# An earlier in-place sum, other banks for the queries, and half of an older head's PV between a query group and its scores

## The chip, the cores and the metric

The kernel runs on one core of a Trainium2 chip. The metric is device time in microseconds (us) of one execution, lower is better. Where I speak of "the trace", it is the hardware profiler's record of one execution.

How to read a line of a timeline: start (us from the beginning of the span), length in us, engine, line of the kernel, operation, what it writes <- what it reads, shapes, number of instructions merged into the line, and in brackets how long the engine was idle before it and what ended that. PE is TensorE's matmuls, PEld its weight loads, DVE is VectorE, ACT ScalarE, POOL GpSimd; SPq issues DMAs from SyncE's queue. A bank is one of the eight banks of PSUM, into which TensorE writes. PV is the product of the probabilities with V. "Start to start" is the distance between the starts of two neighbouring matmuls.

## The reference, cut to what matters

```python
x = A_x                                   # 1 x 2048 x 448, bf16
xn = layernorm(x)
q = xn @ wq                               # 16 query heads of 256
k, v = last 512 positions of the caches   # 8 key heads, each serves 2 query heads
p = softmax(q @ k.T / 16)
s = (p @ v) @ wo
g = silu((gelu(xn @ w_gate) * (xn @ w_up)) @ w_down)
return x + s * g
```

The 2048 rows are worked in four chunks of 512. For the attention that makes 64 steps: step m is query head m mod 16 of chunk m // 16, with key head (m mod 16) // 2. "Head 12" below is step 12.

## The kernel before: the parts that matter

Every operation is planned with the buffers that it reads and writes, and each engine runs its own operations in the order in which they were planned. So a line that stands earlier in this program stands earlier in its engine's queue, and a wait at the head of a queue holds everything behind it.

The gate/up part runs over 56 column blocks, two in each step `n`. Between its matmuls it plans sums for the down product, which is computed from seven products instead of eight and needs sums and differences of the activations (`sum_act`, on VectorE). The sum with k = 0 writes its result into the activations themselves, so the first product of the down stage has to wait for it.

```python
ACT_SUMS = [(n, (c, k, i)) for c, i, ns in ((0, 0, (10, 11, 19, 21)), (0, 1, (23, 23, 25, 25)),
                                            (1, 0, (30, 32, 34, 34)), (1, 1, (36, 36, 38, 38)))
            for k, n in enumerate(ns)]
DOWN_AT = {27: 0, 39: 1}
```

The attention, with cuts:

```python
def q_group(n, pairs, more_act=False):        # queries of two heads, into two pairs of banks
    ...
    group(units, 0, QC, True, True)           # 64-row matmuls, two of them side by side
    for i, b in enumerate(pairs):
        act(qT[:, s, 0, :], bank[b], ...)     # one half copied by ScalarE (ACT)
        ...                                   # the other by VectorE (DVE), or by ACT if more_act

def s_mm(m):                                  # scores of head m, four blocks of 128 rows
    for t4 in range(4):
        ...                                   # two matmuls into bank AB[t4]; exp on ACT
        if t4 % 2 == 1:
            ...                               # reciprocal and two scalings on DVE
            dma_t(pT[:, x, t4 // 2, ...], pn[:, y, ...])    # DMA transpose, on the SP queue

def pv(m):                                    # probabilities times V: two halves of four matmuls
    for e in range(2):
        b = BB[m % 2 * 2 + e]
        mms(... va[:, g, j, e * P:(e + 1) * P], pT[:, x, ...] ...)
        ...                                   # copy of the half: e = 0 on ACT, e = 1 on DVE

groups = [0, 4, 12, 18, 26, 34, 42, 50, 58, 64]     # a query group in front of each of these heads
for m in range(64):
    if m in groups:
        for i in range(m, hi, 2):
            q_group(i, ((cur, nxt[::-1], (cur[1], nxt[1])) if three else (cur, nxt) * 2)[p], end)
            ...
            if m == 12 and p == 0:
                for g in range(6, 8): load_k(g)
                for g in range(5, 8): load_v(g)     # V of the last three key heads
                ...                                 # and loads of x and of the gates, on another queue
    s_mm(m)
    ...
    if len(late) == LAG:                      # LAG = 2: PV of head m - 2 follows the scores of head m
        pv(late.pop(0))
    late.append(m)
```

`cur` are the four banks AB of the scores, `nxt` the four banks BB of PV; between two query groups no one else uses them.

The softmax here doesn't subtract the row's maximum and nothing guards it: scores larger than these inputs give would overflow.

Of the kernel before, what the change touches and what calls it, by code (L numbers as in the profile page):

```python
# [168 lines left out]
def bass_recurrent_scan__sliding_block_cached__geglu_ffn__prompt_kernel(  # L169
# [41 lines left out]
    es = ExitStack()  # L211
    with es:
# [158 lines left out]
        groups = [0, Q0, Q0 + QS, Hq + 2] + list(range(Hq + 2 + QS, NQC * Hq, QS)) + [NQC * Hq]  # L371

        def qs(n):
            g = max(i for i in groups if i <= n)
            return n - g + (QS - Q0 if g == 0 else 0)
# [355 lines left out]
        def sum_wt(o, x, y, i):  # L731
# [6 lines left out]
            (48, (o, x, y, i)) for i in range(NB) for o, x, y in ((5, 2, 4), (6, 5, 0), (3, 1, 5))]  # L738
        WD_CASTS = [(16, (j, e, n, i)) for j, e, n in ((0, 0, 0), (4, 0, 1), (2, 1, 1), (1, 1, 0)) for i in range(2)]
        WD_SUMS = [(18, (4, 4, 0)), (20, (5, 2, 4)), (22, (6, 5, 0)), (24, (3, 1, 5))]  # L740
        ACT_SUMS = [(n, (c, k, i)) for c, i, ns in ((0, 0, (10, 11, 19, 21)), (0, 1, (23, 23, 25, 25)),
                                                    (1, 0, (30, 32, 34, 34)), (1, 1, (36, 36, 38, 38)))
                    for k, n in enumerate(ns)]
        DOWN_AT = {27: 0, 39: 1}
        gu_evac(0, 0)
        gu_evac(1, 2)
# [3 lines left out]
        cur, nxt = (0, 2), (4, 6)  # L750
        for n in range(4, NU, 2):
# [6 lines left out]
            cur, nxt = nxt, cur  # L758
# [24 lines left out]
            if n + 1 in DOWN_AT:  # L783
                def norms():
                    for f in (ln_a, ln_a, ln_b, ln_b):
                        f()
                end = down7(DOWN_AT[n + 1], (cur[0], cur[0] + 1, cur[1], cur[1] + 1, nxt[0], nxt[0] + 1),
                            (g2x[:, 0:2, :], g2x[:, 2:4, :]), b_g2x, then=norms if n < 28 else None)
                end(0, 1)
                end(2, 3)  # L790
                cur, nxt = (nxt[1], cur[1]), (cur[0], nxt[0])
# [10 lines left out]
        def q_group(n, pairs, more_act=False):  # L802

            c, h = divmod(n, Hq)
            units = [(b, lambda j, k, i=i: wq[:, k, (h + i) * Dh + j * P:(h + i) * Dh + (j + 1) * P],
                      wqr[:, h + i, :], slice(c * QC, (c + 1) * QC), b_wql[h // HG][:1], b_wql[h // HG][1:], b_xnT[c * 4:c * 4 + 4])
                     for i, b in enumerate(pairs)]
            group(units, 0, QC, True, True)
            for i, b in enumerate(pairs):
                s = qs(n + i)  # L810
                act(qT[:, s, 0, :], bank[b], ACT.Copy, (b_ps[b],), (b_qT[s][0],))
                if more_act and i:
                    act(qT[:, s, 1, :], bank[b + 1], ACT.Copy, (b_ps[b + 1],), (b_qT[s][1],))
                    continue
                K.op("dve", lambda v, s=s, b=b: v.tensor_copy(qT[:, s, 1, :], bank[b + 1]),  # L815
                     (b_ps[b + 1],), (b_qT[s][1],))

        AB, BB = [], []
        LAG = 2
# [20 lines left out]
                    dma_t(pT[:, x, t4 // 2, :, :, :].rearrange("p t j q -> p (t j) q"),  # L840
                          pn[:, y, :, :].rearrange("p t k -> p (t k)"), (b_pn[y],), (b_pT[x][t4 // 2],))

        def pv(m):
            h = m % Hq
            g, x = h // 2, m % NPT
            for e in range(2):
                b = BB[m % 2 * 2 + e]
                mms([(bank[b].rearrange("p (t q) -> p t q", q=P), va[:, g, j, e * P:(e + 1) * P],
                      pT[:, x, :, :, j, :].rearrange("p a t q -> p (a t) q"), j == 0, j == NJ - 1)
                     for j in range(NJ)], [b_va[g]] + b_pT[x], (b_ps[b],))  # L850
                i = 2 * h + e
                if e == 0 or m >= NS - LAG:
                    act(oTh[:, i, :], bank[b], ACT.Copy, (b_ps[b],), (b_oT[i],), scale=WS)
                else:
                    K.op("dve", lambda v, i=i, b=b: v.tensor_scalar(  # L855
                        oTh[:, i, :], bank[b], WS, None, op0=ALU.mult), (b_ps[b],), (b_oT[i],))
# [131 lines left out]
        late = []  # L988
# [8 lines left out]
        for m in range(NS):  # L997
            if m in groups:
                hi = groups[groups.index(m) + 1]
                three = hi - m == 6  # L1000
                for i in range(m, hi, 2):
                    end = m > Hq and m % Hq == LAG
                    p = (i - m) // 2
                    q_group(i, ((cur, nxt[::-1], (cur[1], nxt[1])) if three else (cur, nxt) * 2)[p], end)
                    if m == 0:
                        sum_act(2, 2 + p)
                    if m == Q0 and p == 0:
                        K.reuse(b_kT[2:6] + b_va[3:5])
                        for g in range(2, 6):
                            load_k(g)  # L1010
                        for g in range(3, 5):
                            load_v(g)
                    if m == Q0 and p < 2:
                        gates3(2 * p)
                        gates3(2 * p + 1)
                    if m == Q0 + QS and p == 0:
                        K.reuse(b_kT[6:] + b_va[5:] + [b for y in b_xr for b in y])
                        for g in range(6, Hkv):
                            load_k(g)
                        for g in range(5, Hkv):  # L1020
                            load_v(g)
                        now = [[o for o in K.ops if o.eng == "pe"][-1]]
                        for t in range(NG2):
                            load_g2(t, now)
                        for t in range(NXR):
                            dma("pool", xr[:, t, :], x_view[:, t, :], (), b_xr[t], now)
                    if end and p:
                        burst_end((m // Hq - 1) * 4 + p - 1)
                    if m > Hq and m % Hq == LAG + QS and p == 1:
                        burst_end((m // Hq - 1) * 4 + 3)  # L1030
                if m == 0:
                    K.reuse([b for x in b_pT for b in x] + b_pn + b_p32)
            if m > Hq and m % Hq == LAG:
                K.reuse(b_pn + b_p32)
            s_mm(m)
            if m < LAG:
                if m == 0:
                    gates2 = down7(2, (BB[0], BB[1], AB[2], AB[3], BB[2], BB[3]), g2w, b_g2w, (3, 4, 6, 5, 2, 1),
                                   lambda: [sum_act(3, k) for k in range(4)])
                else:  # L1040
                    gates3 = down7(3, (BB[1], BB[0], AB[2], AB[3], BB[2], BB[3]), g2w, b_g2w, (3, 4, 2, 5, 6, 1),
                                   lambda: [gates2(q) for q in range(4)])
                    K.reuse(b_pT[2])
                if m == LAG - 1:
                    K.reuse(b_oT + [b for y in b_qT[:QS - Q0] for b in y])
                    assert not CASTS and not SUMS
            if len(late) == LAG:
                pv(late.pop(0))
            if m > Hq and m % Hq == LAG - 1:
                if m // Hq == 1:  # L1050
                    for b in [y for x in b_xs for y in x]:
                        b.old.extend(y for t in range(4) for z in b_xnT[t] for y in z.readers + [z.writer])
                burst(m // Hq - 1)
            late.append(m)
# [56 lines left out]
```

## Time and profile before

| | before |
|---|---|
| three runs, median (range) | 542.15 us (542.05 to 542.58) |
| span of the profiled run | 539.9 us |
| TensorE busy | 532.9 us, 99% |
| VectorE, ScalarE busy | 71%, 58% |
| granted TensorE clock | 1.000 |

A busy share of 99% says that TensorE is the bound, but not that it does useful work all the time: the end of a matmul is modelled, and a short wait between two of them disappears in the overlap. I therefore read start-to-start distances. The lines are shown in the prediction.

### The profile page before, as it was taken

How to read it: one execution, taken by the hardware profiler on the slowest of the kernel's cores; microseconds unless marked ns; L12 is line 12 of the kernel's file. 1: busy time of each engine (PE TensorE's matmuls, PEld its weight loads, DVE VectorE, ACT ScalarE, POOL GpSimd, SP SyncE). 2: the span in 40 equal slices, each digit the busy share in tenths (PEclk: the TensorE clock that was granted, in tenths of full speed). 3: DMA queues.
4: the chain of work that ended last, by engine and by line, in shares of the span. 5: the costliest groups of instructions: out<-in, count | busy, mean ns of one | idle time of the engine just before them, and what ended most of it. 6: DMA issues, size and time to landing. Idle time of an engine off the chain costs nothing.

```text
span 539.9 us, 10920 instructions
## 1 busy us (share of the span) xinstructions
PE 532.9 (99%) x4155; PEld 310.9 (58%) x4180; DVE 383.8 (71%) x839; ACT 314.0 (58%) x782; POOL 40.1 (7%) x78
## 2 busy tenths in 40 slices
PE   9999999999999999999999999999999999999998
PEld 5556657449644444984444469544444984444487
DVE  6689785799767757935875786366667934776785
ACT  5466354873668768116866850488488106876820
POOL 1131120000000010003001000120000003001010
PEclk9999999999999999999999999999999999999999
DMA  9569172942596776302861860067448302772821
GB/s 295 125 186 108 55 124 76 263 101 46 114 186 137 154 186 153 60 1 83 167 141 50 152 137 1 18 156 140 95 106 147 70 1 69 164 158 73 148 66 35
DMA packets 171604, 61.38 MB, mean 114 GB/s; under 512 B 155104, under 2 KB 168416, under 8 KB 171552
## 3 DMA queue, kind: packets, MB, share of 16 engines
q1 hardware_dynamic: 167488, 51.30, 44.5%
q0 software_dynamic: 3008, 8.72, 6.7%
q8 instruction: 33, 0.54, 0.4%
q10 hardware_dynamic: 1056, 0.66, 0.4%
q14 instruction: 19, 0.16, 0.1%
HBM read 19.76 MB, written 3.67 MB: 43 GB/s over the span
## 4 chain that ended last, share of the span: by engine, by line
PE 92%; DVE 2%; ACT 2%; DMA 2%; issue 1%; ACTq 0%
PE bank L394 91%; ACT p L830 2%; DMA pT<-pn 2%; DVE pn L837 1%; PE bank L511 1%; DVE actTh L560 0%; DVE rden L834 0%; DVE wdt L388 0%; PE bank L492 0%; ACT gl L385 0%; DVE actTh L388 0%; DVE sd L388 0%; ACT oTh L385 0%; DVE xnT L884 0%; DVE gl L424 0%
## 5 line engine op out<-in xcount | busy, mean ns | idle before, releaser
L830 ACT ACTIVATE p<-bank 128x512 f32<-128x512 f32 x256 | 150.4, 596 | 28.1 <-DVE pn L837 25.9
L394 PE MATMUL bank<-pT,va 128*128 128x512 bf16 x512 | 120.8, 379 | 0.3
L394 PE MATMUL bank<-kT,qT 128*128 128x512 bf16 x487 | 117.8, 379 | 2.3 <-ACT qT L385 1.0
L837 DVE TENSOR_SCALAR pn<-p,rden 128x512 bf16<-128x512 f32 x256 | 113.0, 484 | 9.1 <-DMA pT<-pn 4.8
L394 PE MATMUL bank<-xnT,wq 64*128 64x512 bf16 x768 | 94.9, 376 | 0.0
L394 PEld LDWEIGHTS bank<-pT,va 128*128 128x128 bf16 x512 | 49.6, 98 | 61.3 <-DMA pT<-pn 2.3
L394 PEld LDWEIGHTS bank<-kT,qT 128*128 128x128 bf16 x512 | 49.3, 98 | 61.7 <-issue 3.4
L394 PE MATMUL bank<-xnT,wgu 64*128 64x512 bf16 (+2 forms) x768 | 84.0, 350 | 0.1
L385 ACT ACTIVATE qT<-bank 128x512 bf16<-128x512 f32 x76 | 44.1, 596 | 51.6 <-PE bank L394 49.9
L815 DVE CAST qT<-bank 128x512 bf16<-128x512 f32 x52 | 34.8, 690 | 49.3 <-PE bank L394 49.3
L394 PEld LDWEIGHTS bank<-xnT,wq 64*128 64x128 bf16 x768 | 36.7, 94 | 46.3 <-ACT p L830 1.7
L394 PEld LDWEIGHTS bank<-xnT,wgu 64*128 64x128 bf16 x768 | 37.7, 94 | 35.8 <-issue 0.6
L834 DVE RECIPROCAL rden<-rsum 128x2 f32<-128x2 f32 x128 | 21.2, 166 | 46.7 <-ACT p L830 46.5
L830 ACT ACTIVATION_READ_ACCUMULATOR p<-bank 128x1 f32 x256 | 51.6, 201 | 0.0
L394 PE MATMUL bank<-wt,sr 128*128 128x224 f16 x512 | 50.0, 259 | 0.0
L394 PEld LDWEIGHTS bank<-wt,sr 128*128 128x128 f16 x512 | 49.0, 98 | 0.4 <-ACT oTh L385 0.2
L385 ACT ACTIVATE gl<-bank 128x512 bf16<-128x512 f32 x56 | 33.0, 596 | 26.4 <-PE bank L394 22.1
L560 DVE TENSOR_TENSOR actTh<-bank,gl 128x512 f16<-128x512 f32 x56 | 37.4, 688 | 11.9 <-PE bank L394 6.4
L855 DVE TENSOR_SCALAR oTh<-bank 128x512 f16<-128x512 f32 x62 | 42.4, 684 | 0.0
L385 ACT ACTIVATE oTh<-bank 128x512 f16<-128x512 f32 x66 | 38.9, 589 | 3.9 <-PE bank L394 3.9
L394 PE MATMUL bank<-wt,oTh 128*128 128x224 f16 (+1 forms) x416 | 38.4, 252 | 0.0
L394 PEld LDWEIGHTS bank<-wt,oTh 128*128 128x128 f16 x416 | 37.2, 98 | 0.9
(77 smaller groups left out, 387.9 us busy)
## 6 DMA issues: line engine op xcount, KB each, us to landing
wtb<-in_A_wo_dram POOLq DMA_DIRECT2D x4, 896.0 KB, 10.5
wq<-in_A_wq_dram SPq DMA_DIRECT2D x2, 1536.0 KB, 8.5
va<-in_A_v_cache_dram SPq DMA_DIRECT2D x8, 256.0 KB, 6.2
pT<-pn SPq DMA_TRANSPOSE x128, 2.8
xr<-in_A_x_dram POOLq DMA_DIRECT2D x15, 112.0 KB, 2.3
wd<-in_B_w_down_dram SPq DMA_DIRECT2D x1, 1568.0 KB, 8.0
g<-g_all POOLq DMA_DIRECT2D x14, 112.0 KB, 2.3
out_dram<-xr POOLq DMA_DIRECT2D x12, 112.0 KB, 2.1
```

The lines of the kernel that those rows point to most:

```text
L385: K.op("act", lambda e, o=o, i=i: e.activation(o, i, func, scale=scale), reads, writes)
L394: ins = e.matmul(o, lhsT=l, rhs=r, start=st, stop=sp, skip_group_check=True)
L511: ins = e.matmul(bank[b][:, 0:w], lhsT=gl[:, 0, 0:P], rhs=gl[:, 0, 0:w], start=True, stop=True)
L560: K.op("dve", lambda e: e.tensor_tensor(actTh[:, c % 2, f, :], bank[b + 1], gl[:, s, :], ALU.mult), (b_ps[b + 1], b_gl[s]), (b_actT[c % 2] ...
L815: K.op("dve", lambda v, s=s, b=b: v.tensor_copy(qT[:, s, 1, :], bank[b + 1]), (b_ps[b + 1],), (b_qT[s][1],))
L830: K.op("act", lambda e, b=b, r=r, z=z: e.activation(p32[:, z, :], bank[b], ACT.Exp, scale=att_scale, accum_out=rsum[:, r:r + 1]), (b_ps[b] ...
L834: K.op("dve", lambda e, r=r: e.reciprocal(rden[:, r - 1:r + 1], rsum[:, r - 1:r + 1]), b_rsum[r - 1:r + 1], b_rden[r - 1:r + 1])
L837: K.op("dve", lambda e, r=r - 1 + t, z=(n - 1 + t) % NP32, y=y, t=t: e.tensor_scalar(pn[:, y, t, :], p32[:, z, :], rden[:, r:r + 1], None, ...
L855: K.op("dve", lambda v, i=i, b=b: v.tensor_scalar(oTh[:, i, :], bank[b], WS, None, op0=ALU.mult), (b_ps[b],), (b_oT[i],))
```

## The change

The intent: take the in-place sum out of the way of the first down product, and give the engines that copy the queries a little more time before the scores come, by putting four PV matmuls of an older head between the two. For that the query groups write other pairs of banks, so that the banks of PV and of the scores are copied out in time.

```diff
-        ACT_SUMS = [... ((0, 0, (10, 11, 19, 21)), (0, 1, (23, 23, 25, 25)),
+        ACT_SUMS = sorted([... ((0, 0, (10, 10, 20, 22)), (0, 1, (16, 24, 26, 26)),
                                 (1, 0, (30, 32, 34, 34)), (1, 1, (36, 36, 38, 38)))
-                    for k, n in enumerate(ns)]
+                    for k, n in enumerate(ns)], key=lambda x: x[0])

-        def pv(m):
+        def pv(m, es=(0, 1)):
...
-            for e in range(2):
+            for e in es:
...
-   q_group(i, ((cur, nxt[::-1], (cur[1], nxt[1])) if three else (cur, nxt) * 2)[p], end)
+   q_group(i, ((cur, nxt[::-1], (cur[1], nxt[1])) if three else
+               (cur, nxt, (cur[0], nxt[0]), (cur[1], nxt[1])) if hi - m == 8 else
+               ((cur[0], nxt[0]), (cur[1], nxt[1])))[p], end)
...
+            split = m in groups and len(late) == LAG
+            if split:
+                pv(late[0], (0,))
             s_mm(m)
...
             if len(late) == LAG:
-                pv(late.pop(0))
+                pv(late.pop(0), (1,) if split else (0, 1))
```

More of the change, by code (lines that the diff above doesn't have):

```diff
@@ L740, in bass_recurrent_scan__sliding_block_cached__geglu_ffn__prompt_kernel @@
         WD_SUMS = [(18, (4, 4, 0)), (20, (5, 2, 4)), (22, (6, 5, 0)), (24, (3, 1, 5))]
-        ACT_SUMS = [(n, (c, k, i)) for c, i, ns in ((0, 0, (10, 11, 19, 21)), (0, 1, (23, 23, 25, 25)),
+        ACT_SUMS = sorted([(n, (c, k, i)) for c, i, ns in ((0, 0, (10, 10, 20, 22)), (0, 1, (16, 24, 26, 26)),
                                                     (1, 0, (30, 32, 34, 34)), (1, 1, (36, 36, 38, 38)))
-                    for k, n in enumerate(ns)]
+                    for k, n in enumerate(ns)], key=lambda x: x[0])
         DOWN_AT = {27: 0, 39: 1}
@@ L1003, in bass_recurrent_scan__sliding_block_cached__geglu_ffn__prompt_kernel @@
                     p = (i - m) // 2
-                    q_group(i, ((cur, nxt[::-1], (cur[1], nxt[1])) if three else (cur, nxt) * 2)[p], end)
+                    q_group(i, ((cur, nxt[::-1], (cur[1], nxt[1])) if three else (cur, nxt, (cur[0], nxt[0]), (cur[1], nxt[1])) if hi - m == 8 else ((cur[0], nxt[0]), (cur[1], nxt[1])))[p], end)
                     if m == 0:
```

## The prediction

> **What bounds the kernel now.** I read the page's busy row, then the chain that ended last, then the timeline at each place where the chain leaves TensorE.
>
> ```profile
> span 539.9 us, 10920 instructions
> PE 532.9 (99%) x4155; PEld 310.9 (58%) x4180; DVE 383.8 (71%) x839; ACT 314.0 (58%) x782; POOL 40.1 (7%) x78
> PE 92%; DVE 2%; ACT 2%; DMA 2%; issue 1%; ACTq 0%
> ```
>
> TensorE is the bound: 99% of the span, 92% of the chain, granted clock 1.000. The other engines count only where TensorE waits for them. So I took the start-to-start distances of all matmul records and marked each one over the usual spacing (216 ns for 512 columns, 107 ns for a 64-row one, two of which run side by side). A record that is missing shows as a doubled distance and is no loss: before the scores there are eight weight loads and seven matmuls. After the first 11 us three kinds of loss are left.
>
> First, the wait ahead of the first chunk's down product:
>
> ```profile
> 48.52 1.48 PE L394 MATMUL bank<-xnT,wgu 64*128 64x512 bf16 x12
> 49.13 0.96 DVE L388 TENSOR_TENSOR wdt<-wdh,wdt 128x1568 f16<-128x1568 f16 x1
> 50.01 0.55 DVE L388 TENSOR_TENSOR actTh<-actTh 128x768 f16<-128x768 f16 x1
> 50.60 0.56 DVE L388 TENSOR_TENSOR sd<-actTh 128x768 f16<-128x768 f16 x1
> 50.62 1.52 PE L394 MATMUL bank<-wdh,actTh 128*128 128x224 f16 x14 [0.63 <-DVE actTh L388]
> ```
>
> The last start before it is 49.60, the next 50.62: 1.005 us. At the second chunk's down product, whose sums are early, the same switch takes 0.308 us. So 1.005 - 0.308 = 0.70 us is real waiting, for the in-place sum at 50.01.
>
> Second, the switch from each query group to the scores:
>
> ```profile
> 391.21 1.46 PE L394 MATMUL bank<-xnT,wq 64*128 64x512 bf16 x12
> 392.06 1.24 ACT L385 ACTIVATE qT<-bank 128x512 bf16<-128x512 f32 x2 [1.78 <-PE bank L394]
> 392.59 1.41 PEld L394 LDWEIGHTS bank<-kT,qT 128*128 128x128 bf16 x8 [0.42 <-issue]
> 392.82 1.67 PE L394 MATMUL bank<-kT,qT 128*128 128x512 bf16 x7 [0.16 <-ACT qT L385]
> 393.24 0.60 ACT L830 ACTIVATE p<-bank 128x512 f32<-128x512 f32 x1
> ```
>
> It names ACT, but the first kT weights load 0.304 us after the last start of the query group (392.289 to 392.593), in every group, as at the down product above, where other operands are read. I take it for the price of going from 64-row to 128-row matmuls, not for a wait on the copies.
>
> Third, PV waiting for its transposed probabilities:
>
> ```profile
> PEld bank L394 <- DMA pT<-pn: 2.3, 5, 0.6
> pT<-pn SPq DMA_TRANSPOSE x128, 2.8
> ```
>
> Per head I measured from the first kT weight load of its scores to the landing of its second transpose and to the first weight load of its PV. An ordinary head: first exp at +0.91, last exp ends +3.52, second transpose issued +4.76, landed +7.48, PV at +8.63: 1.15 us spare. The first head of a group: exp +0.65, landed +7.25, PV +8.43: 1.18 spare. Only about 1.15 us therefore protects PV. In the trace 27 of the 128 transposes take over 3.2 us instead of 2.7, up to 4.67, and 26 of those 27 have a packet of the instruction queues (16 or 8 KB) in flight; of the 101 quick ones 15 have. These hits make the existing waits (heads 28, 39, 47, 61, some 0.2 to 0.5 us each).
>
> **What the Trainium skill says.** "TensorEngine Tiling (Array Packing)", section Key Properties: changing the tiling mode drains TensorE. The trace agrees: 0.30 us start to start from 64-row to 128-row work instead of 0.107, whatever the next operand. "TensorE: Matmul & The Clock Gate", Single matmul latency, gives (398 + N)/2.4 ns; for N = 512 that is 379, and the page has 379. "Runtime: NRT & Kernel Launch", Instruction fetch mechanics, says that instructions are refilled in 16 KiB blocks by a DMA queue; the trace has such packets of 16384 bytes, about 1 us each. "DMA: Bandwidth & Descriptors", Issuing engines are not separate DMA queues: all DMAs interleave on the same 16 engines. That fits the slow transposes; no run yet shows it as a cause.
>
> **The change, part by part.** No work is added or removed: DVE has 635 rows in both orders, TensorE the same matmuls.
>
> *Sums.* The in-place sum (0.55 us, elements 768) leaves the DVE queue just before the down product and goes ten steps up, where DVE has idle pieces of 0.3 to 0.5 us in each 3 us step; another (0.66) moves one step up. TensorE never waits in those steps and a bank comes round again only every second step. The first down product then waits for nothing but the switch: gain 0.70 us. Its sixth and seventh products need sums that DVE ends near 53.5, and come at 55.3 and 56.6, so nothing new waits. As all later work is TensorE after TensorE, the 0.70 us should survive to the end.
>
> *PV half.* In eight groups (heads 4, 12, 18, 26, 34, 42, 50, 58) four PV matmuls go ahead of the scores. That is 4 x 0.216 = 0.864 us of the same work at another place. The mode switch is still there, in front of PV instead of the scores, so I book no gain for TensorE. What moves is the slack. Scores, exps and transposes of the first head come up to 0.864 us later; its PV does not. On ACT the copy of that PV half now stands before the first exp: half ready at +1.03 after the switch, copy 0.55 to 0.59, so ACT is free at +1.65 where the scores would have allowed +1.51. The first exp comes at 0.864 + 0.78 instead of 0.635, about 1.0 us later; with 1.18 spare, 0.17 us is left. So heads 4, 12, 26, 42, 58 still make it, barely, if no fetch falls on them; in the trace of before none does.
>
> Heads 18, 34 and 50 are different. There ACT makes three of the four query copies, so it is late already:
>
> ```profile
> 250.50 1.73 ACT L385 ACTIVATE qT<-bank 128x512 bf16<-128x512 f32 x3 [1.29 <-PE bank L394]
> 252.12 0.61 ACT L830 ACTIVATE p<-bank 128x512 f32<-128x512 f32 x1
> ```
>
> First exp at +1.08. The change absorbs this delay, so they move by 0.59 us only, but these heads now have 0.07, 0.27 and 0.04 us spare, as loads of x and a fetch run beside their transposes (3.43, 3.53 and 4.19 us). If those collide as now, PV waits about 0.5, 0.3 to 0.6 and 0.6 us; if the later issue steps past the other traffic, nothing. I take half to two thirds: 0.9 us in all.
>
> The second head of a group now follows its first after 2.59 us instead of 3.45, while an ordinary head costs DVE 2 x (0.17 + 0.88) + 0.69 = 2.8 us. Following three exp buffers and the in-order DVE queue by hand, its last exp ends some 0.7 us late and the third head's 0.4 late; ordinary heads leave ACT 0.26 us idle, so the delay is gone by the fifth. Their spare time stays above 0.4 us, but a fetch at head 20 or 28 costs more: 0.2 us more together.
>
> *New banks.* In groups of eight the third pair takes half of the banks that the second pair has just filled. They are wanted 0.86 us into the third pair; the copies need up to 0.7 us and began 0.6 before its start. Only in head 4's group, where gates stand in front of them on DVE (copy 153.60 to 154.28, wanted at 154.27), do I book 0.08 us.
>
> Sum: -0.70 + 0.08 + 0.9 + 0.2 = +0.5 us by the middle of each term, from -0.6 (no collision) to +1.4.
>
> **Rivals.**
> A: only the sum counts: the PV half is neutral, all transposes land in time. For it: 1.15 us spare in ordinary heads. Against it: the three heads with under 0.3 us. 541.4.
> B: the split pays: the 0.30 us at the switch is partly a wait for the query copies, as the row's label says, and PV, whose banks are free, hides it: eight times up to 0.2 us, so 542.15 - 0.7 - 1.6 = 539.9. Against it: the same 0.30 at places that read no query copies, and a label that names an ACT operation done long before.
> C: the softmax chain cannot catch up: each group keeps 0.86 us of lateness and PV waits for it, 8 x 0.86 = 6.9 us, 548.4. Against it: ACT's 0.26 and DVE's 0.7 us of idle per head.
> D: fetches fall otherwise because everything shifts by some tenths: +-0.5 us either way.
>
> **Range and chances.** By my sum 542.15 + 0.5 = 542.6; the collisions are the part I trust least and rival A's 541.4 is nearly as likely, so I put the time between them, at 542.0. 8 times in 10 between 541.1 and 543.1: the low end is all of the gain and fewer hits on the transposes, the high end three full waits and a few fetches more. 2% is 10.8 us; only C comes near it: faster 0.01, same 0.98, slower 0.01.
>
> **What would show it.** The down product starts about 0.31 us after the last gate/up matmul. The switch behind each query group stays at 0.30 us, now in front of PV weights; a shorter one proves B. The first exp of heads 4, 12, 26, 42, 58 comes about 1.0 us after where it was relative to the switch, with 0.1 to 0.3 us left before PV, and waits on the transposes appear at heads 18, 34, 50 and nowhere in the other first heads. The prediction is wrong if waits on transposes grow by over 2 us in all, if they vanish, or if the gain of the sum turns up as a later wait in the same down product.

## The result, and the profile after

The changed kernel took 545.75 us in the median of six runs (543.53 to 547.95), the kernel before 542.21 us in its six (541.93 to 542.61). The ratio is 1.0063, with a 95% interval of 1.0034 to 1.0092. A ratio here is the mean time of one kernel's fast runs over that of the other's in the same rounds, so it is not quite the ratio of the medians. In this call the change made the kernel slower by more than half a percent (0.2% and 0.4% in two later calls, see the experiments); I had predicted 542.0 and a range of 541.1 to 543.1.

The page of the profiled run after, an execution of 544.81 us:

```profile
span 543.0 us, 10912 instructions
PE 534.0 (98%) x4155; PEld 310.4 (57%) x4180; DVE 382.6 (70%) x839; ACT 314.2 (58%) x782; POOL 40.0 (7%) x78
PE 89%; DVE 4%; DMA 3%; ACT 2%; issue 1%; SPq 0%; DVEq 0%; ACTq 0%
```

TensorE has the same 4155 matmuls on record and is still the bound, but 3% less of the chain is its own. What took its place is small change: DVE, DMA. Such a page doesn't say where 3 us went. This does: I cut both traces at the points where TensorE changes from one kind of work to another (first weight load of each stage) and subtracted the lengths. 24 of the 33 stages agree within 0.02 us. The others are in these rows:

| stage, by its first weight load | before | after | difference |
|---|---|---|---|
| start of the first down product | 50.62 | 50.27 | -0.35 |
| query group of head 0 | 6.38 | 6.56 | +0.18 |
| scores of head 0 | 1.53 | 2.24 | +0.71 |
| query group of head 12, up to the first weight load behind it | 9.17 | 10.86 | +1.69 |
| waits within the attention stages, over their shortest length | 0.76 | 1.62 | +0.86 |
| everything else | 471.46 | 471.48 | +0.02 |
| span | 539.92 | 543.03 | +3.11 |

(Shortest length: the 128-weight-load stages take 27.73 us before a query group and 27.43 before the output product, the 96-load ones 20.52, in every trace in which no wait is seen in them.)

So the difference is accounted for to a few hundredths, and it comes from four places. One by one.

**The sum: as predicted.** The timeline of the kernel after, at the first down product:

```profile
48.86 1.48 PE L394 MATMUL bank<-xnT,wgu 64*128 64x512 bf16 x12
49.48 0.96 DVE L388 TENSOR_TENSOR wdt<-wdh,wdt 128x1568 f16<-128x1568 f16 x1
50.27 0.94 PE L394 MATMUL bank<-wdh,actTh 128*128 128x224 f16 x8
50.36 0.55 DVE L388 TENSOR_TENSOR sd<-actTh 128x768 f16<-128x768 f16 x1
```

The DVE sum into `actTh` is gone from this place (it now runs at 37.79), and the distance from the last gate/up start to the first down start is 0.309 us instead of 1.005. The start at 50.27 is only 0.35 us earlier, not 0.70, because the first loads of the kernel came later in this execution: in the traces of the other kernels with this sum (one with a changed warm-up left out) it lies between 49.89 and 50.54.

**Head 12: a wait that I had not seen.** First the timeline before, at the end of head 12's query group, then after:

```profile
195.16 1.46 PE L394 MATMUL bank<-xnT,wq 64*128 64x512 bf16 x12
196.78 1.67 PE L394 MATMUL bank<-kT,qT 128*128 128x512 bf16 x7 [0.16 <-issue]
198.29 0.38 PE L394 MATMUL bank<-pT,va 128*128 128x512 bf16 x1
```

```profile
195.80 1.46 PE L394 MATMUL bank<-xnT,wq 64*128 64x512 bf16 x12
196.65 1.24 ACT L385 ACTIVATE qT<-bank 128x512 bf16<-128x512 f32 x2 [1.78 <-PE bank L394]
198.87 0.56 PEld L394 LDWEIGHTS bank<-pT,va 128*128 128x128 bf16 x4 [2.11 <-issue]
198.90 0.81 PE L394 MATMUL bank<-pT,va 128*128 128x512 bf16 x3 [1.64 <-issue]
```

TensorE stands still for 1.64 us in front of the PV half of head 10. "issue" means that the profile found nothing that released it. Head 10 needs V of key head 5, and the three last V loads are issued just then:

```profile
192.98 1.98 SPq L379 DMA_DIRECT2D va<-in_A_v_cache_dram  x3
```

By the trace's record of landings, the first of the three landed at 198.81, and PV's first weights were loaded at 198.87. In the kernel before it landed at 197.52 and PV came at 198.07, behind the scores: 0.55 us in time. The change brought this PV forward by the length of the scores, 1.73 us, and so in front of its own operand.

**Head 0: two waits for the new banks.** The timeline of the kernel before, at the scores of head 0, where nothing comes between them and the down product:

```profile
118.20 1.41 PEld L394 LDWEIGHTS bank<-kT,qT 128*128 128x128 bf16 x8 [0.46 <-DVE qT L815]
118.66 1.08 DVE L388 TENSOR_TENSOR sd<-sd,actTh 128x1792 f16<-128x1792 f16 x1
119.66 1.28 DVE L815 CAST qT<-bank 128x512 bf16<-128x512 f32 x2
119.73 1.46 PEld L394 LDWEIGHTS bank<-wdh,actTh 128*128 128x128 f16 x14
```

The timeline of the kernel after, at the query group of head 0 and its scores:

```profile
112.00 1.34 DVE L560 TENSOR_TENSOR actTh<-bank,gl 128x512 f16<-128x512 f32 x2
112.75 0.33 PEld L394 LDWEIGHTS bank<-xnT,wq 64*128 64x128 bf16 x6 [0.53 <-DVE actTh L560]
...
118.31 1.08 DVE L388 TENSOR_TENSOR sd<-sd,actTh 128x1792 f16<-128x1792 f16 x1
...
119.31 1.28 DVE L815 CAST qT<-bank 128x512 bf16<-128x512 f32 x2
...
120.04 0.11 PEld L394 LDWEIGHTS bank<-kT,qT 128*128 128x128 bf16 x2 [1.03 <-DVE qT L815]
```

The first pair of this group now takes two of the banks BB, in which the last gate/up results still lie; TensorE waits for DVE's product at 112.00. The second pair takes two of the banks AB; DVE copies them out only at 119.31, because a sum of 1.08 us stands before the copy in its queue, and the last block of head 0's scores wants bank AB[3]. Before the change the second pair lay in BB alone, which nobody wanted before the next stage: there the same copy comes just as late (119.66), and the scores do not wait for it.

**Transposes.** The chain of waits, weight loads on transposes, after:

```profile
PEld bank L394 <- DMA pT<-pn: 4.1, 8, 0.7
```

And the first heads of the group at 18, in the timeline after:

```profile
260.29 1.89 PE L394 MATMUL bank<-kT,qT 128*128 128x512 bf16 x8
262.40 0.82 PE L394 MATMUL bank<-pT,va 128*128 128x512 bf16 x3 [0.22 <-DMA pT<-pn]
```

PV of head 18 now waits for its transpose, and so does PV of heads 34 and 50; start to start these take 0.60, 0.51 and 0.58 us instead of 0.22. The first heads 4, 12, 26, 42 and 58 have 0.24 to 0.30 us left. A caution on this view: its 4.1 us (2.3 before) is idle time of the weight loader, which runs ahead of the matmuls. What TensorE lost is the 1.62 (0.76) of the table. Start to start it is made up of heads 18, 34 and 50 (1.04) and of heads 7, 20 and 51 (0.08, 0.19 and 0.23, each with a slow transpose); the waits of before at heads 39, 47 and 61 (0.29, 0.30 and 0.12) are gone.

### The profile page after: what moved, and what is told of

Its sections match the earlier page's. It is cut to its first block, busy times and chain, and to the rows that moved or that the text cites.

```text
span 543.0 us, 10912 instructions
## 1 busy us (share of the span) xinstructions
PE 534.0 (98%) x4155; PEld 310.4 (57%) x4180; DVE 382.6 (70%) x839; ACT 314.2 (58%) x782; POOL 40.0 (7%) x78
## 3 DMA queue, kind: packets, MB, share of 16 engines
HBM read 19.76 MB, written 3.67 MB: 43 GB/s over the span
## 4 chain that ended last, share of the span: by engine, by line
PE 89%; DVE 4%; DMA 3%; ACT 2%; issue 1%; SPq 0%; DVEq 0%; ACTq 0%
PE bank L394 89%; DMA pT<-pn 2%; DVE wt L388 1%; ACT p L830 1%; DVE pn L837 1%; DVE actTh L560 1%; DMA x<-in_A_x_dram 1%; ACT qT L385 1%; DVE qT L815 0%; ACT oTh L385 0%; DVE rden L834 0%; DVE sd L388 0%; DVE actTh L388 0%; SPq L379 0%; DVE oTh L855 0%
## 5 line engine op out<-in xcount | busy, mean ns | idle before, releaser
L394 PE MATMUL bank<-pT,va 128*128 128x512 bf16 x512 | 122.2, 379 | 2.3 <-issue 1.6
```

Of the source, the lines that this page charges most:

```text
L394: ins = e.matmul(o, lhsT=l, rhs=r, start=st, stop=sp, skip_group_check=True)
```

## The experiments

My theory after the result: the loss is three separate costs of the reordering, the V load (1.7), the banks of head 0 (0.9) and PV's shorter time for its transposes (about 0.9), against a gain of 0.7 from the sum. The rival to it: the PV half itself, by making the scores later, costs wherever it stands, and repairing one wait only moves it. Of 14 kernels that went to the chip, 14 gave a result, in four calls; kernels of one call ran on one chip and share runs of the kernel before. Times are medians of five or six runs, with their range. In traces I give the same quantities as above: "Q12" is the query group of head 12 up to the next weight load (9.17 us before), "head 0" its two stages together (7.91 before), "waits" the sum of waits in the attention stages (0.76 before).

| kernel | time (range) | ratio to before (95%) | Q12 | head 0 | waits |
|---|---|---|---|---|---|
| changed, first | 545.75 (543.53 to 547.95) | 1.0063 (1.0034 to 1.0092) | 10.86 | 8.80 | 1.62 |
| after_again | 543.55 (542.80 to 545.88) | 1.0023 (1.0001 to 1.0046) | 10.42 | 8.81 | 0.93 |
| sums_only | 541.80 (541.07 to 542.34) | 0.9984 (0.9963 to 1.0006) | 9.17 | 7.91 | 1.62 |
| v5_early | 542.96 (542.37 to 543.72) | 1.0009 (0.9990 to 1.0028) | 9.17 | 8.81 | 1.10 |
| old_banks_head0 | 543.78 (541.70 to 545.78) | 1.0020 (0.9994 to 1.0047) | 10.20 | 7.91 | 0.97 |
| both_mended, fast runs | 541.21 to 543.06 | 0.9994 (0.9981 to 1.0007) | slow trace | | |
| no_split_old_banks0 | 540.83 (540.60 to 541.58) | 0.9974 (0.9961 to 0.9987) | 9.17 | 7.91 | 1.26 |
| fetch_moved | 542.88 (542.23 to 543.04) | 1.0008 (0.9996 to 1.0020) | 9.17 | 7.91 | 1.67 |
| scores_ahead (faulty) | 937.33 | 1.7294 | | | |
| sums_only2 | 541.35 (541.07 to 542.51) | 0.9995 (0.9983 to 1.0008) | 9.17 | 7.91 | 0.73 |
| both_mended2 | 541.41 (541.37 to 541.87) | 0.9994 (0.9980 to 1.0007) | 9.17 | 7.91 | 1.39 |
| mended_no_end | 542.14 (540.97 to 543.08) | 1.0007 (0.9994 to 1.0020) | 9.17 | 7.91 | 2.21 |
| scores_ahead2 | 541.83 (541.65 to 542.39) | 1.0001 (0.9989 to 1.0014) | 9.17 | 7.91 | 1.19 |
| after_third | 544.59 (543.78 to 546.09) | 1.0038 (1.0021 to 1.0055) | 10.28 | 8.81 | 3.06 |
| v5_late | 548.72 (548.28 to 551.17) | 1.0109 (1.0091 to 1.0128) | 13.95 | 8.81 | 5.09 |

The three traced quantities say more than the times. Q12 and head 0 are the same to 0.01 us wherever the same code stands and no load is waited for; the scatter of the times is a us or two. For all traces at clock 1.000, the span less the start of the first down product, Q12, head 0 and waits is 471.5.

### after_again: the changed kernel once more

> The changed kernel once more, as the reference of this call. Its first six times lie between 543.5 and 548.0, against 541.9 to 542.6 of before. My theory: the scatter is the landing of the V load of key head 5, for which the PV half in front of head 12's scores now waits 1.7 us in the one profile taken. Then the profile here has this wait again, between 1 and 5 us, and a run's time goes with it. Rival: the scatter is the time of slow transposes all over the attention; then the wait at head 12 is 1.7 us again and the rest of the difference lies elsewhere. Median 543.5 to 547.

The wait at head 12 came again, 1.25 us over the 9.17, so it is no accident of one execution. The median of 543.55 is inside what I expected. One run took 545.88 at a mean granted clock of 0.997, the others 542.8 to 544.0.

### sums_only

```diff
 before, and only:
-  (0, 0, (10, 11, 19, 21)), (0, 1, (23, 23, 25, 25))
+  (0, 0, (10, 10, 20, 22)), (0, 1, (16, 24, 26, 26))      # sorted by step
```

> Only the earlier in-place sum, everything else as before. Theory: 0.70 us less before the first down product, nothing lost later: 541.5, ratio 0.9987, scatter as small as before's (0.6 us). Rival: with everything 0.7 us earlier the fetches of instructions hit other transposes, and up to 0.5 us of it is given back: 541.5 to 542.2.

The first down product starts at 49.94 instead of 50.62, and all stages up to head 18 have the length of before: 0.67 us are carried that far. Then 1.23 us are lost in the stage of heads 18 to 25: the second transpose of head 19 took 5.24 us, with two fetches of instructions in flight beside it, and PV waited. So more was given back in this execution than the rival of this expectation allowed. The median is 541.80.

### v5_early: is it the V load?

```diff
 in the group of head 4, behind its gates:
+                        if p == 1:
+                            K.reuse(b_va[5:6])
+                            load_v(5)
 in the group of head 12:
-                        for g in range(5, Hkv):
+                        for g in range(6, Hkv):
                             load_v(g)
```

> The changed kernel, but the V of key head 5 is loaded one query group earlier (after the gates of head 4's group). Theory: the wait between the query group and the PV half at head 12 falls from 2.02 us start to start to the bare switch, 0.31, and the kernel gains at least 1.7 us on the changed kernel of this call, 542 to 543.2, with a scatter under 1 us. Rival (the PV half itself is late there, or its query copies are not done): the gap at head 12 stays over 1 us.

The timeline at the same place as above, of this kernel:

```profile
195.48 1.46 PE L394 MATMUL bank<-xnT,wq 64*128 64x512 bf16 x12
196.87 1.04 PE L394 MATMUL bank<-pT,va 128*128 128x512 bf16 x4
197.74 0.59 PE L394 MATMUL bank<-kT,qT 128*128 128x512 bf16 x2
```

The wait is gone, Q12 is 9.17 again, and no later stage took it back. The rival falls here: nothing but the load held this PV half. In time, the kernel gained 0.6 us in the medians against the changed kernel of the same call and not the 1.7 at least that I expected: this call's trace of the changed kernel had only 1.25 us to give there. Between the two profiled runs the gain is 1.15 us (543.52 to 542.37): 1.25 at head 12, less 0.17 more in the waits on transposes, and 0.07 at the start. That the medians differ by 0.6 only is scatter of the other runs, as far as I can tell. All six times lie within 1.4 us, and none over 543.72.

### v5_late: the same cost, made larger

```diff
 changed kernel, in the group of head 12:
-                        for g in range(5, Hkv):
+                        for g in range(6, Hkv):
                             load_v(g)
+                        load_v(5)
```

> The changed kernel with the suspected cost made larger: V of key head 5 is issued third instead of first of the three V loads. In the changed kernel's trace the third one landed 2.9 us after the first. Theory: the query group of head 12 with the wait behind it grows from 10.4 to 10.9 us to about 12.8 to 13.8, and the kernel by 2.3 to 3 us against the changed kernel of this call. Rival (the PV half waits for something else there): no change.

Q12 grew to 13.95 us, a little more than the 12.8 to 13.8 expected, and the time by 4.1 us in the medians against the changed kernel of the same call, outside the 2.3 to 3 that I expected. Between the two profiled runs it is 5.82 us of span: 3.67 of Q12, 2.11 in the stage behind it, and 0.05 from the start and the other waits together. Over five kernels, the landing of this load and the first PV weight load behind the query group, in us:

| kernel | V of key head 5 lands | first weights of PV |
|---|---|---|
| changed, first | 198.81 | 198.87 |
| after_again | 198.12 | 198.18 |
| after_third | 197.79 | 197.85 |
| old_banks_head0 | 197.38 | 197.45 |
| v5_late | 201.59 | 201.65 |

PV follows the landing by 0.06 to 0.07 us each time. The surplus in the stage behind shows in the timeline and in the table of stretches of this kernel (columns of the second: stretch, its length, busy time and count of TensorE, weight loads, DVE, ACT, GpSimd, then the granted clock, the DMA share and GB/s):

```profile
201.68 1.86 PE L394 MATMUL bank<-pT,va 128*128 128x512 bf16 x4 [4.74 <-issue]
203.76 2.76 PE L394 MATMUL bank<-kT,qT 128*128 128x512 bf16 x7 [0.22 <-issue]
```

```profile
196.00:198.00 2.00, 0.94 (x10) 0.20 (x6) 1.34 (x2) 1.19 (x2) 0.00 (x0) 1.00 1.09 312
200.00:202.00 2.00, 0.32 (x1) 0.14 (x2) 0.00 (x0) 0.00 (x0) 0.00 (x0) 0.50 0.04 12
206.00:208.00 2.00, 2.00 (x11) 0.91 (x10) 1.57 (x5) 1.38 (x5) 0.00 (x0) 1.00 0.00 0
```

In these 4.74 us without a matmul the granted clock falls to half. By the clock record it falls at 199.12, 2.2 us after the end of the last matmul, and is full again at 205.94, 6.8 us later, of which 4.3 are matmul time at half speed; the stage behind lost 2.1 us by it. The Trainium skill describes this ("TensorE: Matmul & The Clock Gate", section What's actually happening: the array goes to half rate after an idle window of some 3.4 us and comes back after as much sustained work), and this trace agrees in kind; its own figures are 2.2 us without a matmul before the fall, and 4.3 us of matmuls before the return. The wait of 1.64 us in the changed kernel's first trace left the clock at 1.00. All six runs of this kernel have a mean clock of 0.994 to 0.997. That makes a long wait on this bound engine dearer than its length.

### old_banks_head0

```diff
 changed kernel, first query group:
-   ... if hi - m == 8 else ((cur[0], nxt[0]), (cur[1], nxt[1])))[p], end)
+   ... if hi - m == 8 else (cur, nxt))[p], end)
```

> The changed kernel, but the first query group (four heads) keeps the old pairs of banks. Theory: the two new waits there go, on the DVE copy of a gate/up bank before the second pair (0.31 us, of which 0.18 lost) and inside the scores of head 0 on the DVE copy of the query behind a long sum (0.71 us): 0.9 us less than the changed kernel of this call. Rival: the waits come from the sums, which stand at the same place in both; then they stay and the time is the same within 0.2 us.

Timeline of the end of head 0's query group and its scores, of this kernel:

```profile
116.05 1.46 PE L394 MATMUL bank<-xnT,wq 64*128 64x512 bf16 x12
117.48 1.90 PE L394 MATMUL bank<-kT,qT 128*128 128x512 bf16 x8
119.21 1.03 PE L394 MATMUL bank<-wdh,actTh 128*128 128x224 f16 x9
```

All eight score matmuls in one go, and the down product behind them 1.73 us later instead of 2.44. Head 0's stages have 7.91 us again: 0.90 less, both waits gone. The sums stand at the same steps in both kernels, so the rival falls. In the times nothing of it can be seen (543.78 against 543.55, ratios 1.0020 and 1.0023): the runs spread from 541.70 to 545.78, the highest again at a clock of 0.997 (this kernel still has the V wait). What was expected of the time failed.

### both_mended and both_mended2

Both edits together, twice the same kernel.

> The changed kernel with both repairs: V of key head 5 loaded a group earlier and the old bank pairs in the first query group. Theory: the costs are separate and add, so the stages up to head 12 are 1.69 + 0.90 us shorter than in the changed kernel's trace, and what is left against before is the gain of the sum (-0.70) and the waits on transposes at heads 18, 34 and 50 and their followers (+0.3 to +1.2): 541.6 to 542.8. Rival (the PV half loses elsewhere too, by late scores): still over 543.

Four of its runs took 541.21 to 543.06. The fifth, the profiled one, took 804.43 at a clock of 0.655 in all of its length. It counts as slow and is left out; I don't know its cause, and no other run shows it.

> Both repairs again, for a trace at full clock (the one before fell on a run at clock 0.655 throughout). Theory: query group of head 12 at 9.17 us and head 0's stages at 6.38 and 1.53 as before the change, and only the attention stages that start with heads 18, 34 and 50 longer than with the sums alone in most draws; the first heads of the groups have 0.25 to 0.3 us left before PV. Time 541.2 to 543.1, 0.3 to 0.8 us over the sums alone.

541.41 us, within 0.1 of the sums alone in the same call (541.35), where I had expected 0.3 to 0.8 more. Stages as expected. The waits are 1.39 us here against 0.73: heads 18, 34 and 50 wait again, and 0.39 falls in head 4's stage; in return 0.29 us which the sums alone lose at the end of the stage of heads 42 to 49 are not lost. So with both repairs the PV half gains nothing, and in this call it costs nothing in time. The call before says otherwise: there the four fast runs of both_mended have a mean of 541.99, the five of no_split_old_banks0, which has no half, 541.01. Whether the half in itself costs up to 1 us is therefore open; refuted is only that repairing one wait moves it to another place of the same length.

### no_split_old_banks0

```diff
 changed kernel with the old pairs of head 0, and:
-            split = m in groups and len(late) == LAG
+            split = False
```

> The sums and the new bank pairs in the groups of eight, but no PV half ahead of the scores, and old pairs in the first group. Theory: the new pairs cost at most 0.1 us, the query groups of 112 weight loads stay at 12.19 us, PV has again 1.15 us before it at the first heads: 541.2 to 542.2, as with the sums alone. Rival (the pairs of the groups of eight cost too): query groups over 12.3 us.

The query groups of eight heads take 12.19 us as before: the new pairs cost nothing there. The time, 540.83 us and a ratio of 0.9974, is the best of all. By the stages it is the same as the sums alone, apart from where the waits on transposes fall (1.12 us in the stage of heads 50 to 57, 0.14 at heads 18 to 25); I take the difference between 540.8 and 541.8, which were measured in different calls, for such draws, not for a merit of the pairs; that is not shown.

### fetch_moved: are the slow transposes made by fetches of instructions?

```diff
 the sums alone, and:
-        warm(9, 2, QC)          # 9 warm-up matmuls of 512 columns
+        warm(36, 2, QC // 4)    # 36 of 128
```

> The sums alone, and the 9 warm-up matmuls of 512 columns replaced by 36 of 128: the same time, 54 TensorE instructions more ahead of everything. If fetches of TensorE's instructions (the 16384-byte packets) make the transposes slow, each such packet comes about 54 instructions earlier, 5.8 us in the attention, and the slow transposes move with it: those around 260, 303, 375, 415, 459 and 503 us go to about 254, 297, 369, 409, 453 and 498, and the heads that wait change. If the slow transposes come from the transfers of the attention itself (a place in the program), they stay at heads 19, 28, 39, 47, 50 and 60. Time 541 to 543 either way.

The warm-up turned out 1.1 us longer (first down product at 51.03); that part of the expectation was wrong. The 16384-byte packets moved: from 260.0, 303.4, 375.4, 415.1, 459.2 and 503.7 us to 254.8, 300.3, 368.7, 412.7, 455.7 and 501.1, though the kernel itself runs 0.4 to 1.6 us later at these points. The slow transposes went with them in four of the six cases (issued at 298.5 and 299.9, 366.9 and 368.3, 410.2 and 411.7, 499.2 and 500.7, each with the packet in flight). At 254.8 no transpose was in flight; two at 459.2 and 460.7 were slow without a packet, which stays unexplained. The heads that wait changed: head 5, which never waited before, now does (its stage lost 0.49 us), and the 1.23 us at heads 18 to 25 shrank to 0.06. The place in the program is the same, only the fetches moved. So the fetches are a cause of slow transposes, no longer a coincidence, though not the only one. Counted over traces, a packet of the instruction queues is in flight during 31 of 33 transposes over 3.2 us in the changed kernel, 24 of 24 with the sums alone, 28 of 31 here; the few others ran beside loads of x, as far as I can tell. Of the some 100 quick transposes of each trace 14 to 20 have such a packet in flight as well, mostly one of 8192 bytes; of those with a packet of 16384 bytes, 18 of 21 were slow with the sums alone and 19 of 23 here.

### mended_no_end

```diff
 both repairs, and:
-            split = m in groups and len(late) == LAG
+            split = m in groups and len(late) == LAG and m % Hq != LAG
```

> Both repairs, and no PV half ahead of heads 18, 34 and 50. Theory: these heads have their old 0.04 to 0.3 us left instead of a wait of 0.3 to 0.4, so up to 1 us less than both repairs, 541 to 542.3. Rival (fetches decide, not the half): no difference beyond the scatter of 0.5 us.

A miss: it should have had the smaller waits and had 2.21 us of them, of which 1.69 fell in the stage of heads 18 to 25, where no PV half stood in front. The second transpose of head 19 took 5.71 us there, with two packets of instructions in flight. The theory held where it spoke: heads 18, 34 and 50 did not wait at all and had 0.12, 0.06 and 0.19 us left. For the time the rival was right: one draw of the fetches weighed more than what these three heads saved.

### scores_ahead and scores_ahead2: the reverse of the change

If PV suffers from too little time for its transposes, the other direction should help: the first two score blocks of the next head ahead of PV.

```diff
 the sums alone, and (scores_ahead2):
-            s_mm(m)
+            s_mm(m, (2, 3) if ahead else (0, 1, 2, 3))
+            ahead, held = m >= LAG and m + 1 < NS and m + 1 not in groups, []
+            if ahead:
+                s_mm(m + 1, (0, 1), held)      # its transpose is kept back
 ...
                 pv(late.pop(0))
+            for turn in held:
+                turn()                         # and issued behind this PV
```

> The sums alone, and the reverse of the change: the first two score blocks of the next head go ahead of PV, so that PV comes 0.86 us later against its own scores instead of earlier. Theory (PV has 1.15 us before it, a fetch takes 0.7 to 2.5): spare time of ordinary heads about 2.0 us, waits of PV on transposes from 2 to 3 us down to under 0.5: 539.0 to 540.5, faster than both. Rival (the softmax chain of ACT and DVE is what limits, or the banks of the scores come free too late): TensorE waits for ACT before scores instead, and the time is 541.5 or more.

My first version was wrong. It issued the transpose of head m + 1 before PV of head m - 2, into the same of the three buffers, so PV waited for it and then read the wrong probabilities. Both checks, for races and against the reference, let it pass; the second presumably because its tolerance doesn't notice. Its 937 us are a lesson on plan order, nothing else. In the second version an assertion at build time makes sure that each PV reads its own head.

> The reverse of the change, mended: the earlier version issued the first transpose of the next head into a buffer that the older PV had still to read, so PV waited 6.6 us in every head for wrong data (its 937 us say nothing of the idea). Here that transpose is issued after this PV. Theory: ordinary heads have 2.0 us before PV instead of 1.15, waits of PV on transposes fall from 2 to 3 us to under 0.7: 539.0 to 540.6, faster than both kernels. Rival (exps and banks of the scores then limit): TensorE waits on ACT before scores, 541.5 or more.

The chain of waits of scores_ahead2, three of its lines on weight loads:

```profile
PEld bank L394 <- ACT p L832: 3.7, 9, 0.5
...
PEld bank L394 <- ACT oTh L385: 1.4, 4, 0.4
...
PEld bank L394 <- DMA pT<-pn: 0.8, 1, 0.8
```

The mechanism is as I thought: ordinary heads have up to 2.6 us left before PV, and a single wait on a transpose remains. The time is not: 541.83 us, no better than the sums alone. In part new waits came, on ACT before the second head's scores in the groups of 18, 34 and 50 (0.23 us each). But the larger error was the size of the prize. I had put it at 2 to 3 us from the weight loader's idle time; by stages, the sums alone lose only 0.73 us to all waits in the attention in the trace of this call. This order turned that into 1.19, of which 0.43 is the one wait that is left, on a transpose of 5.20 us.

### sums_only2

> The sums alone once more, as the reference of this call and for a narrower interval: 541.1 to 542.3, ratio 0.997 to 0.9995.

541.35 us, ratio 0.9995 with an interval that includes 1. With the first call and the closely related no_split_old_banks0 that makes three ratios of 0.9984, 0.9995 and 0.9974, of which only the last has an interval clear of 1. The gain of 0.7 us, 0.13%, is plain in the stages and hardly larger than the scatter of the times.

### after_third

> The changed kernel a third time. Its first call gave 543.5 to 544.8 in three executions and 546.7 to 548.0 in three others, its second call 542.8 to 545.9. If the wait for the V load of key head 5 depends on the chip or on the draw, the profile here has it at another length than 1.25 or 1.69 us, and a profile over 545 us shows it above 3 us. If the high times come from something else, such a profile has 1.0 to 1.7 us there and the rest elsewhere. Median 543 to 547.

A profile of 545.30 us, just over the mark that I had set, has 1.11 us at head 12 and not over 3, and 3.06 us of waits in the attention, the most of any trace of this kernel (1.1 each at heads 19 and 47, whose transposes took up to 4.6 and 5.2 us). So the V wait is a steady 1.0 to 1.7 us in four traces, and it is the waits on transposes that make a run of this kernel 1 to 2 us longer or shorter.

## Why the prediction was wrong

Point by point, by the prediction's own steps.

**The sum: right.** 0.70 us expected, 1.005 to 0.309 us start to start measured, and carried on in the stages behind. (A slip in the working: the sum went up by four turns of the gate/up loop, not ten. It is without effect on the result.)

**The mode switch: right.** The distance behind the query groups of eight stayed 0.308 us, now in front of PV's weights; behind that of head 12 too, once V was there (v5_early). Rival B is refuted: there was nothing to hide at the switch.

**"What moves is the slack": here it failed.** The prediction followed the scores, exps and transposes of the new head and said that its PV doesn't move. It never asked whether the PV half that does move, that of the head two before, has its operands 1.73 us earlier. For seven of the eight groups it has. At head 12 its V is in flight: it had 0.55 us to spare in the kernel before, as the landings in that trace would have told. Measured: 1.03 to 1.69 us in the four traces of this code with the V load in its old place; v5_early takes it away and v5_late makes it 4.78, with PV 0.06 to 0.07 us behind the landing wherever it was held.

**"New banks": the group that pays was left out.** I booked 0.08 us for head 4's group and looked at the groups of eight alone. That group shows no loss (12.19 us in every trace), and the first group of four, whose banks change too, lost 0.90 us in all three draws of the changed kernel. old_banks_head0 takes exactly this away.

**The transposes: right in kind, near in size, but a draw.** The first heads kept 0.24 to 0.30 us where I had 0.17. Heads 18, 34 and 50 wait as foreseen: over the usual spacing 0.38, 0.30 and 0.36 us, 1.04 together, for a booked 0.9. In each of the six traces with the half in all groups and no clock loss all three wait, 0.3 to 1.0 us together; without the half and with PV in its old order they wait 0 to 0.24 us together, but for one trace with 1.1 at head 50. The whole term came to +0.86 for a booked 1.1 in the pair of traces that I compared. That the sum is so near is luck: other heads added 0.50, for a booked 0.2, and the waits of before at heads 39, 47 and 61 (0.71 together) fell away, as the fetches fell elsewhere, which is rival D. (The "some 0.2 to 0.5 us each" of the prediction at heads 28, 39, 47 and 61 is idle time of the weight loader; start to start TensorE lost 0.02, 0.29, 0.30 and 0.12 there.) Yet over all traces the total can't be told from the scatter. The six traces have 0.93 to 3.06 us of waits (mean 1.51); the kernel before and three with the early sum and no half have 0.73 to 1.62 (mean 1.09; fetch_moved, left out for its other warm-up, has 1.67).

**The sum of it.** Put the two measured terms for the missing ones into the prediction's own working, 542.6 us: less 0.08, plus 0.90 and 1.69, gives 545.1. The first six runs gave 545.75 in the median. I had moved my estimate from 542.6 down to 542.0 for rival A; that was also in the wrong direction.

**What stays open.** Three of the first six runs lie at 546.7 to 548.0 and were not profiled. One of them has a mean clock of 0.996, which fits a wait long enough to halve the clock, as v5_late shows it. Over the whole record, three of the 24 runs of code with the half and the V load in its old place have a clock of 0.996 or 0.997 (and all six of v5_late 0.994 to 0.997); of the runs without the V wait none has one under 0.999, the faulty kernel and the one slow run apart. That a long V wait happened in these three is argued, not shown. The two at 546.7 have a clock of 1.000. A draw of waits such as after_third's, with the V wait at its upper end, comes to within a us or so of them; no trace shows one.

## The version to keep

Keep the earlier sum and leave the PV where it was: 541.80 and 541.35 us in two calls, against 542.14 and 541.95 of the kernel before in the same calls, and 540.83 against 542.30 with the new pairs in the groups of eight. Against the kernel before, the gain is plain in the stages; in the times only the last of the three is clear of noise. The PV half with both repairs reaches the same in one call (541.41) for more code, and not in the other.

## What to carry to other kernels

When an operation is moved forward, list everything that it reads and when each of these arrives, not only the operand that used to be late; a load that had half a microsecond to spare doesn't show in the profile of before as a wait. When banks or buffers are exchanged, go through every group that uses them, the odd-sized ones first. And cut two traces at the same points of the program and subtract: here that gave four causes and a remainder of 0.02 us, where run times scattered over 2 us and the page's "issue" named nobody.

## What the Trainium skill lacked or had wrong

- "TensorE: Matmul & The Clock Gate", Back-to-back issue gap: this section says that in a real stream of weight loads and matmuls 512 columns come every 131 ns, and that N/2.4 + 2.5 (216 ns) is for isolated ones. The runs show 216 ns for each matmul in long streams with a weight load before every one, at clock 1.000.
- "TensorEngine Tiling (Array Packing)", Key Properties: it says that a change of mode drains TensorE, not what that costs. In every trace it is 0.31 us start to start from 64-row to 128-row work (0.20 lost), and 0.31 instead of 0.22 in the other direction (0.10 lost).
- "Runtime: NRT & Kernel Launch", Instruction fetch mechanics: it calls the cost of crossing a block boundary mostly hidden. No loss of TensorE's own shows at these packets (what is left after the four places is 471.5 us in every trace), but the kernel's own DMAs lose: with a 16 KiB packet of about 1 us in flight, DMA transposes of 2.7 us mostly took 3.2 to 5.7, and moving the fetches moved four of six groups of slow transposes (fetch_moved). The size of this cost is on no page that I read.
- "TensorE: Matmul & The Clock Gate", What's actually happening: it gives at least one idle window of some 3.4 us before half rate. Here less was enough: the clock record fell 2.2 us after the end of the last matmul in v5_late, and 1.9 us after it in the shortest of the 53 falls in the trace of the faulty scores_ahead.
